# The query scratch as 16 long rows, and an exp that puts its scores back in order

## The chip, the cores and the metric

The kernel runs on one core of one Trainium2 chip. The metric is the device time of one execution in microseconds (us); lower is better. A core has five engines with queues of their own: PE (matmuls; its weight loads are shown as PEld), DVE (vector), ACT (activation functions), POOL (general purpose, and the issuer of DMAs that cast) and SP (here it only issues DMAs). Sixteen DMA engines serve all queues. The working memory SBUF and the matmuls' output memory PSUM both have 128 partitions.

## The reference, cut to what matters

Two steps follow one another. The first is an attention with pooled keys: `kv` is averaged over 4x4 squares, giving 768 rows per batch, and multiplied by `w_sr`; the result serves as keys and as values.

```python
kv_pool = kv.reshape(B, H // r, r, W // r, r, C).mean(axis=(2, 4))     # r = 4
k = v = kv_pool.reshape(B, -1, C) @ w_sr
s = q @ k.transpose(0, 2, 1) / sqrt(C)                                 # softmax over 768 keys
x = softmax(s) @ v
```

Here B = 4, C = 128, and q has 12,288 tokens per batch. The second step is a mixture of adapters on the 49,152 rows of x: a gate of 8 columns picks two experts per row with softmax weights, and each picked expert adds `w * (x @ A[e]) @ B[e]`, of rank 16.

## The kernel before

The 49,152 tokens are cut into 96 chunks of 512 (`k`), and four chunks make a group of 2048 tokens (`g`, 24 of them). Token p*16+j of a group (p from 0 to 127, j from 0 to 15) belongs to output partition p; chunk m of the group holds j = 4m to 4m+3. So every chunk is four blocks (`s`) of 128 tokens, and a store writes 2 KB in a row per partition.

For the scores PE needs q transposed: channels on the partitions, tokens along the row. Groups 0 and 1 are transposed by PE itself (`turn_q`). For groups 2 to 23, `cast_q(g)` (L78, its DMA on L80) has POOL issue a DMA that reads 1 MB of q in fp32 and writes it as bf16 into a scratch `qbf` in HBM, and `load_qT(g)` (L83, its DMA on L90) has SP issue a transposing DMA from the scratch into the tile `qT`; the last four groups go into a spare tile named `qTs`. Before the change the scratch is an image of q, [2048 tokens, 128], read as 128 rows of 2048 elements; the transpose leaves column j*128+p of `qT` for token p*16+j.

Per chunk there are three units (`scores(k, r)`, L286): two matmuls of 512 columns into one of two PSUM tiles `sg`, then one exp on ACT (L294) of 1024 elements per partition into `em` in fp16. `em[k]` has six blocks of keys (j) by 512 tokens. `attend(k, s)` (L296) then loads 128 tokens of `em` as weights, six times, and multiplies by the values `vx` into the single PSUM tile `acc`. DVE divides by the sum (`normalize`, L315 and L320, giving `xn`). DVE's MAX8 (`top`, L340) finds the two best experts, POOL works out the gates (`route`, L352 to L358; `gates`, L365 to L368, with a tanh on ACT and the tile `gw` as result), PE projects down (`h_ps`), DVE multiplies by the gates (`gate`, L420, giving `hg`), PE projects up (`d_ps`), DVE adds (`finish`, L433) and SP stores (L434). Between these, x and hg are transposed, by PE (`tt_ps`, copied to `tts` by DVE on L389) or, from chunk 68 on, by transposing DMAs on a tile `turn` (L407).

All engines keep the order in which the program is written. It is written in slots, one per chunk: an opening listed step by step in a string, then a loop from slot 8. `begin(k)` (L468) starts a slot: it calls `load_qT` where the table `loads` says so (slot 4g-6 for groups 4 to 17), `cast_q` where `casts` says so, and the loads of the next batch's `kv`. From slot 13 on a slot k computes the three score units of chunk k and attends chunk k-1. The casts and transposes of groups 2 and 3 belong to the opening's step `late` (`cast_first`, L449): POOL waits for an earlier load, casts both, and SP transposes both. In the opening, chunk 8, the first of group 2, is first used by the step `sc 8 0`, which follows `down 1` and precedes `at 4 2`.

All matmuls are recorded under one line, L69, that of the helper `mm`.

Of the kernel before, what the change touches and what calls it, by code (L numbers as in the profile page):

```python
# [11 lines left out]
BF16 = mybir.dt.bfloat16  # L12
U16 = mybir.dt.uint16
FP16 = mybir.dt.float16
AF = mybir.ActivationFunctionType
# [5 lines left out]
def kernel(  # L21
# [10 lines left out]
    nc = tc.nc  # L32
    P = 128
    B, N, C = q.tensor.shape
# [3 lines left out]
    J = NKV // P  # L38
    T = 512
    S = T // P  # L40
    GC = 4
    GT = GC * T
    VC = C + E - 1
    VE = VC + 1
    VP = 2 * C
    NB = N // T
    NCHUNK = B * NB
    scale = 1.0 / float(np.sqrt(C))
# [6 lines left out]
    ppool = ctx.enter_context(tc.tile_pool(name="ppool", bufs=8))  # L55
# [5 lines left out]
    qdram = ctx.enter_context(tc.tile_pool(name="qdram", bufs=1, space=bass.MemoryType.DRAM))  # L61
# [4 lines left out]
    keep = tc.keep_in_program_order  # L66

    def mm(*a, **k):
        return keep(nc.tensor.matmul(*a, **k))  # L69
# [5 lines left out]
    NG = N // GT  # L75
    q_bf, qT, kvr, spare = {}, {}, {}, {}

    def cast_q(g):  # L78
        t = qdram.tile([GT, C], BF16, tag=f"q{g}", name=f"qbf{g}")
        keep(nc.gpsimd.dma_start(t, q[g // NG, (g % NG) * GT:(g % NG + 1) * GT]))  # L80
        q_bf[g] = t

    def load_qT(g):  # L83
        if g < B * NG - GC:
            t = qpool.tile([P, GT], BF16, tag="qT", name="qT")
        else:
            if "q" not in spare:
                spare["q"] = kvpool.tile([P, 4, 2, 4 * C], FP32, tag="kvr", name="qTs")
            t = spare["q"][:, g % GC].rearrange("p x c -> p (x c)").bitcast(BF16)
        keep(nc.sync.dma_start(t.rearrange("c (j p) -> c j p", p=P),  # L90
                               q_bf[g].rearrange("(p j) c -> p (j c)", p=P), transpose=True))
        qT[g] = t


# [113 lines left out]
    kfT, vx = {}, {}  # L208
# [73 lines left out]
    em, acc, xn, xg, srt, gw = {}, {}, {}, {}, {}, {}  # L282
# [3 lines left out]
    def scores(k, r):  # L286
        b = k // NB
        if k not in em:
            em[k] = ppool.tile([P, J, T], FP16, tag="em", name="em")
        rhs = qT[k // GC][:, (k % GC) * T:(k % GC + 1) * T]  # L290
        ps = ps_s.tile([P, 2, T], FP32, tag="sg", name="sg")
        for i in range(2):
            mm(ps[:, i], kfT[b][:, 2 * r + i], rhs, start=True, stop=True)
        keep(nc.scalar.activation(em[k][:, 2 * r:2 * r + 2], ps, AF.Exp, bias=0.0, scale=scale))  # L294

    def attend(k, s):  # L296
        b = k // NB
        if s == 0:
            acc[k] = ps_a.tile([P, S, 256], FP32, tag="acc", name="acc")
        o = acc[k][:, s, 0:VE]  # L300
        for j in range(J):
            mm(o, em[k][:, j, s * P:(s + 1) * P], vx[b][:, j, 0:VE], start=(j == 0),
               stop=(j == J - 1))

    def attend_part(k, r):
        if r == 0:
            acc[k] = ps_a.tile([P, S, 256], FP32, tag="acc", name="acc")
        for s in range(S):
            for j in (2 * r, 2 * r + 1):
                mm(acc[k][:, s, 0:VE], em[k][:, j, s * P:(s + 1) * P], vx[k // NB][:, j, 0:VE],  # L310
                   start=(j == 0 and s % 2 == 0), stop=(j == J - 1 and s % 2 == 1))

    def normalize(k):
# [135 lines left out]
    def cast_first():  # L449
        keep(nc.gpsimd.tensor_copy(late, q_f[1, 2][:, 0, 0:1]))  # L450
        for g in (2, 3):
            cast_q(g)
        for g in (2, 3):
            load_qT(g)
# [3 lines left out]
    def unit(k=None, r=None):  # L458
        k, r = units.pop(0 if k is None else units.index((k, r)))
        scores(k, r)  # L460
# [7 lines left out]
    def begin(k):  # L468
        nonlocal sums, rest
        b, i = divmod(k, NB)  # L470
        g = k // GC
        if k in loads:
            load_qT(loads[k])
        if k in casts:
            cast_q(4 + casts.index(k))
        if b + 1 < B:
            lo = 3 if b == 0 else 0
            if i == lo:
                sums, rest = prepare(b + 1, nc.gpsimd)
                sums = sum(sums, [])  # L480
            if lo <= i < 12 + lo:
                load_kv(b + 1, (i - lo) // 4, (i - lo) % 4, None)
        if k == 7:
            for _ in range(2):
                sums.pop(0)()
# [11 lines left out]
    enter, t, left = {}, 1, list(range(NCHUNK - 3))  # L497
# [10 lines left out]
    def step(op, *w):  # L508
        v = [int(x) if x.isdigit() else engines.get(x, pools.get(x)) for x in w]
        if op == "T":  # L510
            turn_rows(v[0], 2 * (v[2] // 2) if w[1] == "s" else v[2],
                      v[2] % 2 if w[1] == "s" else v[3])
        elif op == "turn":
            turn_q(v[0] // GC, v[0] % GC, *v[1:])
        elif op in ("keys", "keys2", "values"):
            first_rest[v[0]][("keys", "keys2", "values").index(op)]()
        elif op == "gates":
            later.pop(0)()
        else:
            {"spin": spin, "proj1": project, "proj2": project2, "sum": add_rows, "sc": unit,  # L520
             "late": cast_first, "cast": cast_weights, "slot": begin, "at": attend, "atp": attend_part,
             "norm": normalize, "top": top, "route": route, "tr": transposes, "down": down,
             "gate": gate, "up": up, "fin": finish}[op](*v)
# [23 lines left out]
    for k in range(k1, NCHUNK):  # L547
        b, i = divmod(k, NB)
# [11 lines left out]
        if kx and not kd and all(x_ in by_dma for x_ in kx):  # L560
# [16 lines left out]
            for u_ in ku:  # L577
                up(u_)
                finish(u_)
            attend(ka[0], 0)  # L580
            attend(ka[0], 1)
            unit()
            for n in kn:
# [92 lines left out]
    def part(k, o, js):  # L676
        for s in range(S):
            for j in js:
                mm(o[:, s, 0:VE], em[k][:, j, s * P:(s + 1) * P], vx[k // NB][:, j, 0:VE],
                   start=(j == 0 and s % 2 == 0), stop=(j == J - 1 and s % 2 == 1))  # L680

    def wide(o):
# [40 lines left out]
    up_into(K - 4, bank(ps_m))  # L723
    o95 = bank(ps_s).rearrange("p a (b c) -> p (a b) c", c=256)
    part(K, o95, range(4))
    fetch(xT, K - 2)
    tanhs()
    down_into(K - 2, ps_m)
    carry(K - 4)
    normalize(K - 1)  # L730
    turn_x(K - 1, ps_m)
    part(K, o95, range(4, J))
    turn_h(K - 3, ps_a)
    fetch(xT, K - 1)
# [96 lines left out]
```

## Time and profile before

| what | value |
|---|---|
| median of 3 runs | 380.49 us (380.42 to 380.88) |
| profiled execution, span from first to last instruction | 379.1 us |
| PE busy | 368.8 us, 97% |
| DVE busy | 307.6 us, 81% |
| ACT busy | 293.3 us, 77% |
| POOL busy | 217.8 us, 57% |
| DMA moved | 82.22 MB in 93,863 packets |
| mean granted PE clock | 0.995 |

The profiled execution's own time is the span; the median of the runs is 1.4 us more, which lies around the span. A row of a group reads: line, engine, operation, out<-in with shapes, count, then busy time, mean time of one in ns, and idle time of the engine just before. A row of the timeline reads: start in us, length in us, engine, line, operation, count of merged instructions, and in brackets the idle time before it and what ended it. A row of the waits reads: who waited for whom, us in total, times, longest.

### The profile page before, as it was taken

Reading aid. Unit: us, or ns where it says so; the run is one execution under the profiler, and the core shown is the slowest. Engines: PE = TensorE matmul, PEld = TensorE weight load, DVE = VectorE, ACT = ScalarE, POOL = GpSimd, SP = SyncE. Lnnn points to the kernel's source line nnn. Section 1 sums busy time; section 2 is a strip of 40 time slices with the busy share of each in tenths; the row PEclk is TensorE's granted clock in tenths of the full one; section 3 lists DMA queues with packets and bytes.
Section 4 is the critical chain, followed back from the end, with each engine's and each line's share of the span. In section 5 each row is a group of like instructions: output and inputs, shape, how many; then the busy total and the mean of one; then the engine's idle time right before and its main releaser. Section 6 shows DMA issues by size and latency. Waiting matters only on the chain.

```text
span 379.1 us, 11473 instructions
## 1 busy us (share of the span) xinstructions
PE 368.8 (97%) x4448; PEld 292.5 (77%) x4448; DVE 307.6 (81%) x925; ACT 293.3 (77%) x368; POOL 217.8 (57%) x493
## 2 busy tenths in 40 slices
PE   8899999999999999999999999999999999999993
PEld 5577788788788887878788887878787777777782
DVE  1447799998989889898989888898988777777785
ACT  1448986776878788787878787777778999999873
POOL 0120468878732387777833267777675666666442
PEclk9999999999999999999999999999999999999998
DMA  7988979999999998997898998989955867777623
GB/s 247 388 291 151 279 184 266 340 224 241 152 213 228 299 278 268 255 235 165 171 201 226 288 239 245 306 233 198 217 137 140 169 163 153 150 205 168 141 86 140
DMA packets 93863, 82.22 MB, mean 217 GB/s; under 512 B 73104, under 2 KB 73872, under 8 KB 93456
## 3 DMA queue, kind: packets, MB, share of 16 engines
q1 hardware_dynamic: 92672, 69.75, 69.8%
q0 software_dynamic: 704, 11.54, 17.0%
q8 instruction: 35, 0.57, 0.6%
q10 hardware_dynamic: 432, 0.20, 0.2%
q14 instruction: 20, 0.16, 0.2%
HBM read 50.53 MB, written 36.70 MB: 230 GB/s over the span
## 4 chain that ended last, share of the span: by engine, by line
PE 91%; DMA 4%; DVE 2%; issue 1%; ACT 1%; SPq 0%; POOL 0%; ACTq 0%; DVEq 0%; POOLq 0%
PE acc L69 35%; PE sg L69 32%; PE tt_ps L69 8%; PE d_ps L69 5%; PE h_ps L69 5%; DMA kvr<-in_kv_dram 4%; PE kpT_ps L69 2%; PE v_ps L69 1%; DVE kvr L135 1%; DVE xn L320 1%; PE kfT_ps L69 1%; DMA out_dram<-osb 1%; PE qT_ps L69 0%; SPq L102 0%; PE tail_ps L69 0%
## 5 line engine op out<-in xcount | busy, mean ns | idle before, releaser
L294 ACT ACTIVATE em<-sg 128x1024 f16<-128x1024 f32 x288 | 282.4, 1022 | 66.8 <-PE sg L69 64.1
L69 PE MATMUL acc<-vx,em 128*128 128x136 f16 x2280 | 166.5, 223 | 0.0
L69 PEld LDWEIGHTS <-em 128*128 128x128 f16 x2304 | 145.2, 98 | 7.7 <-DVE xn L320 0.4
L69 PE MATMUL sg<-qT,kfT 128*128 128x512 bf16 x480 | 142.1, 379 | 0.8 <-ACT em L294 0.7
L320 DVE TENSOR_TENSOR xn<-acc,rinv 128x540 f32<-128x540 f32 x95 | 68.4, 720 | 3.3
L69 PEld LDWEIGHTS <-tts 128*128 128x128 bf16 x564 | 43.0, 98 | 31.6 <-issue 0.4
L223 POOL TENSOR_TENSOR kvr<-kvr 128x512 f32<-128x512 f32 x54 | 67.3, 1270 | 0.1
L352 POOL TENSOR_TENSOR over<-xn,srt 128x64 f32<-128x64 f32 (+1 forms) x120 | 30.9, 278 | 55.4 <-DVE srt L340 55.3
L433 DVE TENSOR_TENSOR osb<-d_ps,xn 128x512 f32<-128x512 f32 x91 | 62.5, 688 | 0.0
L420 DVE TENSOR_TENSOR hg<-h_ps,gw 128x512 bf16<-128x512 f32 x71 | 49.0, 691 | 6.3 <-POOL gw L368 1.2
L389 DVE COPY tts<-tt_ps 128x1024 bf16<-128x1024 bf16 (+1 forms) x73 | 49.0, 672 | 0.0
L69 PEld LDWEIGHTS <-kfT 128*128 128x128 bf16 x576 | 45.3, 98 | 2.7 <-issue 1.0
L315 DVE RECIPROCAL rinv<-acc 128x4 f32<-128x4 f32 x95 | 17.3, 182 | 36.9 <-PE acc L69 35.9
L367 POOL TENSOR_TENSOR gw<-th,over 128x64 f32<-128x64 f32 (+1 forms) x60 | 17.3, 288 | 49.6 <-ACT th L365 47.4
L69 PEld LDWEIGHTS <-xn 128*128 128x128 bf16 x296 | 22.5, 98 | 16.7 <-DVE xn L320 0.4
L340 DVE MAX8 srt<-xn 128x8 f32<-128x8 f32 x380 | 34.4, 152 | 0.1
L69 PE MATMUL sg<-qTs,kfT 128*128 128x512 bf16 x96 | 28.6, 379 | 0.0
L69 PE MATMUL tt_ps<-id_bf,xn 128*128 128x128 bf16 x284 | 27.4, 219 | 0.0
L69 PE MATMUL h_ps<-a_bf,tts 128*128 128x128 bf16 x284 | 27.4, 219 | 0.0
L69 PE MATMUL tt_ps<-id_bf,hg 128*128 128x128 bf16 x280 | 27.1, 219 | 0.0
L69 PE MATMUL d_ps<-b_bf,tts 128*128 128x128 bf16 x276 | 26.7, 219 | 0.1
L358 POOL TENSOR_SCALAR over<-over 128x64 f32<-128x64 f32 (+1 forms) x60 | 19.8, 330 | 5.4
(93 smaller groups left out, 280.7 us busy)
## 6 DMA issues: line engine op xcount, KB each, us to landing
out_dram<-osb SPq DMA_DIRECT2D x94, 256.0 KB, 4.3
kvr<-in_kv_dram SPq DMA_DIRECT2D x45, 512.0 KB, 7.8
qbf<-in_q_dram POOLq DMA_DIRECT2D x22, 512.0 KB, 7.7
qf<-in_q_dram SPq DMA_DIRECT2D x8, 256.0 KB, 7.4
kvr<-in_kv_dram SPq DMA_DIRECT2D x6, 256.0 KB, 7.8
out_dram<-osb SPq DMA_DIRECT2D x3, 128.0 KB, 2.3
turn<-turn SPq DMA_TRANSPOSE x23, 3.1
qT<-qbf SPq DMA_TRANSPOSE x18, 7.4
```

What stands on the lines that cost most here:

```text
L69: return keep(nc.tensor.matmul(*a, **k))
L223: keep(adder.tensor_tensor(u[:, lo:hi], u[:, lo:hi], v[:, lo:hi], op=ALU.add))
L294: keep(nc.scalar.activation(em[k][:, 2 * r:2 * r + 2], ps, AF.Exp, bias=0.0, scale=scale))
L315: keep(nc.vector.reciprocal(ri, acc[k][:, :, VC]))
L320: keep(nc.vector.tensor_tensor(x[:, :, 0:VC], acc[k][:, :, 0:VC], ri.unsqueeze(2).broadcast_to([P, S, VC]), op=ALU.mult))
L340: keep(nc.vector.max(srt[k0][:, m, s], xn[k][:, s, C:C + E]))
L352: keep(eng.tensor_tensor(d, lg, so[:, :, i].unsqueeze(2).broadcast_to([P, n, 8]), op=ALU.subtract))
L358: keep(eng.tensor_scalar(mask, mask, 0.0, None, op0=ALU.is_ge))
L367: keep(eng.tensor_tensor(w[:, 0:n], th, mask, op=ALU.mult))
L389: keep(nc.vector.tensor_copy(sb[:, lo:hi], ps[:, lo:hi]))
L420: keep(nc.vector.tensor_tensor(hg[k].rearrange("p s (e r) -> p (s e) r", e=E), hp[k].rearrange("p s (e r) -> p (s e) r", e=E), gw[k0][:, m ...
L433: keep(nc.vector.tensor_tensor(osb, dp[k], xn[k][:, :, 0:C], op=ALU.add))
```

## The change

The scratch is written in another order. It is a tile of 16 rows by 16,384 elements: row r holds the tokens whose p is r modulo 16, ordered by chunk m, then by p div 16 (`u`, 8 values), then by block s. The cast therefore writes pieces of 4 tokens, 512 elements. The transposing DMA reads these 16 rows in one instruction, and column (m, u, s, r) of `qT` holds the token. Within a chunk the 128 tokens of one block s no longer lie side by side, but in 8 runs of 16. The matmuls of the scores take the 512 columns as they come; the exp reads its PSUM tile in the order s, then key block and u, then r, and writes `em`, which now has the layout [s, key block, 128 tokens]. So `attend` loads the same 128 tokens as before, from another place in `em`. For groups 0 and 1, still transposed by PE, the exp reads whole blocks of 128 in the order s, key block.

```diff
     def cast_q(g):
-        t = qdram.tile([GT, C], BF16, tag=f"q{g}", name=f"qbf{g}")
-        keep(nc.gpsimd.dma_start(t, q[g // NG, (g % NG) * GT:(g % NG + 1) * GT]))
+        t = qdram.tile([16, GT // 16 * C], BF16, tag=f"q{g}", name=f"qbf{g}")
+        src = q[g // NG, (g % NG) * GT:(g % NG + 1) * GT].rearrange(
+            "(u r m s) c -> r m u (s c)", r=16, m=GC, s=S)
+        keep(nc.gpsimd.dma_start(t.rearrange("r (m u x) -> r m u x", m=GC, x=S * C), src))
         q_bf[g] = t
...
-        keep(nc.sync.dma_start(t.rearrange("c (j p) -> c j p", p=P),
-                               q_bf[g].rearrange("(p j) c -> p (j c)", p=P), transpose=True))
+        keep(nc.sync.dma_start(t.rearrange("c (m r) -> c m r", r=16), q_bf[g], transpose=True))
         qT[g] = t
...
     def scores(k, r):
         b = k // NB
         if k not in em:
-            em[k] = ppool.tile([P, J, T], FP16, tag="em", name="em")
+            em[k] = ppool.tile([P, S, J, P], FP16, tag="em", name="em")
...
-        keep(nc.scalar.activation(em[k][:, 2 * r:2 * r + 2], ps, AF.Exp, bias=0.0, scale=scale))
+        o = em[k][:, :, 2 * r:2 * r + 2]
+        if k // GC > 1:
+            o = o.rearrange("p s i (u r) -> p s (i u) r", r=16)
+            i_ = ps.rearrange("p i (u s r) -> p s (i u) r", s=S, r=16)
+        else:
+            i_ = ps.rearrange("p i (s t) -> p s i t", s=S)
+        keep(nc.scalar.activation(o, i_, AF.Exp, bias=0.0, scale=scale))
...
-            mm(o, em[k][:, j, s * P:(s + 1) * P], vx[b][:, j, 0:VE], start=(j == 0),
+            mm(o, em[k][:, s, j], vx[b][:, j, 0:VE], start=(j == 0),
                stop=(j == J - 1))
```

The two other places that load `em`, `attend_part` and `part`, change in the same way.

More of the change, by code (lines that the diff above doesn't have):

```diff
@@ L309, in attend_part @@
             for j in (2 * r, 2 * r + 1):
-                mm(acc[k][:, s, 0:VE], em[k][:, j, s * P:(s + 1) * P], vx[k // NB][:, j, 0:VE],
+                mm(acc[k][:, s, 0:VE], em[k][:, s, j], vx[k // NB][:, j, 0:VE],
                    start=(j == 0 and s % 2 == 0), stop=(j == J - 1 and s % 2 == 1))
@@ L678, in part @@
             for j in js:
-                mm(o[:, s, 0:VE], em[k][:, j, s * P:(s + 1) * P], vx[k // NB][:, j, 0:VE],
+                mm(o[:, s, 0:VE], em[k][:, s, j], vx[k // NB][:, j, 0:VE],
                    start=(j == 0 and s % 2 == 0), stop=(j == J - 1 and s % 2 == 1))
```

## The prediction

> **What bounds the kernel now.** I read the page's head first, then the busy time by stretch, then the waits, and last the timeline at the places that the change touches.
>
> ```profile
> span 379.1 us, 11473 instructions
> PE 368.8 (97%) x4448; PEld 292.5 (77%) x4448; DVE 307.6 (81%) x925; ACT 293.3 (77%) x368; POOL 217.8 (57%) x493
> DMA  7988979999999998997898998989955867777623
> ```
> ```profile
> core 0: us, PE busy (x) PEld busy (x) DVE busy (x) ACT busy (x) POOL busy (x), PEclk, DMA share, GB/s
> 27.00:60.00 33.00, 32.94 (x393) 26.23 (x392) 26.02 (x91) 28.36 (x35) 13.41 (x27) 1.00 0.83 217
> 60.00:284.00 224.00, 224.00 (x2836) 181.46 (x2834) 200.43 (x581) 173.95 (x209) 145.38 (x271) 1.00 0.99 233
> 284.00:356.00 72.00, 71.92 (x869) 55.80 (x867) 55.01 (x183) 67.28 (x89) 46.05 (x155) 1.00 0.72 162
> ```
> ```profile
> ACT em L294 <- PE sg L69: 52.4, 64, 1.3
> POOL gw L367 <- ACT th L365: 38.7, 32, 2.0
> DVE rinv L315 <- PE acc L69: 30.8, 70, 0.9
> ```
>
> From 27 to 356 us PE is busy in 328.86 of 329 us, at the full granted clock; the other engines wait for it (the last fence is the waits of 60 to 356 us; among them none is PE's own). The DMA engines are nearly as full (0.99 from 60 to 284 us), but nothing on PE waits for them there. The change takes no instruction from PE: the scores' matmuls read 512 neighbouring columns of qT as before, and the attend loads 128 neighbouring fp16 of em as before. So inside those 329 us nothing can be gained; the change can only be hidden or cost. The idle PE time lies ahead of 27 us, where only chunks turned by PE run, and behind 356 us, when all scratch has been read.
>
> **The exp.** It reads 1024 scores per partition in runs of 16 instead of in a row, and writes runs of 256.
>
> ```profile
> L294 ACT ACTIVATE em<-sg 128x1024 f16<-128x1024 f32 x288 | 282.4, 1022 | 66.8 <-PE sg L69 64.1
> L433 DVE TENSOR_TENSOR osb<-d_ps,xn 128x512 f32<-128x512 f32 x91 | 62.5, 688 | 0.0
> L420 DVE TENSOR_TENSOR hg<-h_ps,gw 128x512 bf16<-128x512 f32 x71 | 49.0, 691 | 6.3 <-POOL gw L368 1.2 <-PE kfT_ps L69 0.5
> ```
>
> No ACT instruction here reads in a permuted order. The nearest rows are DVE's: the gate multiply L420 walks its operands in runs of 16, one of them a repeated gw, and takes 691 ns for 512 elements; the plain add L433 takes 688. By that pair 3 ns per 512, so 6 ns per exp. The bounds: -0.02 us (an even walk over the two banks could save a little, nothing suggests more) to +0.25 us, if a run of 16 cost a quarter more; I take +0.01, the end that a measured pair supports. What a dearer exp costs is read where ACT is fullest.
>
> ```profile
> 202.85 2.85 ACT L294 ACTIVATE em<-sg 128x1024 f16<-128x1024 f32 x3 [0.61 <-PE sg L69]
> 204.04 0.59 PE L69 MATMUL sg<-qT,kfT 128*128 128x512 bf16 x2
> 305.87 3.15 ACT L294 ACTIVATE em<-sg 128x1024 f16<-128x1024 f32 x3
> 308.91 0.22 ACT L365 ACTIVATE th<-over 128x32 f32<-128x32 f32 x1
> 309.03 1.02 ACT L294 ACTIVATE em<-sg 128x1024 f16<-128x1024 f32 x1
> ```
>
> Three exps back to back take 2.85, so one starts (2.85-1.02)/2 = 0.915 us after the other. From 284 to 356 us a slot is 309.03-305.87 = 3.16 us and holds three exps and a tanh, 3x0.915+0.12 = 2.87 us: 0.29 us are free, 0.10 per exp. In the slots before, the first exp of a triple ends at 202.85+1.02 = 203.87, and the matmul that wants its PSUM buffer (there are two) starts at 204.04: 0.17 us free. So +0.01 us is hidden, and the price starts at about +0.10. Cost: 0.
>
> **The casts.** The 22 casts (L80) move the same bytes, but write 512 pieces of 1 KB, each from 2 KB of q.
>
> ```profile
> q1 hardware_dynamic: 92672, 69.75, 69.8%
> q0 software_dynamic: 704, 11.54, 17.0%
> ```
> ```profile
> L80 POOL DMA_DIRECT2D qbf<-in_q_dram x22: 504/577/755, 27.0 to 242.4; - x22
> ```
>
> The 704 packets of q0 are 32 per cast, two for each of 16 engines; I read them as one of data and one that ends it, so data goes from 16 pieces to 512. On the DMA engines a cast now holds 0.17x379.1/22 = 2.9 us of all sixteen. An engine gets 32 pieces for one; an average hardware packet, bytes included, is 0.698x16x379.1/92672 = 46 ns, so at most 1.5 us per cast, at least 0 (below it, if short pieces let other queues in sooner). Since that packet's bytes are already in the 2.9, I take a third, 0.5 us: 11 us in all, 3% of the span, on engines that PE does not wait for.
>
> On POOL the issue takes 577 ns, and what is queued behind it are the gates' steps, on which DVE's gate multiply waits.
>
> ```profile
> 95.06 0.36 POOL L358 TENSOR_SCALAR over<-over 128x64 f32<-128x64 f32 x1
> 95.38 0.57 POOL L80 DMA_DIRECT2D qbf<-in_q_dram  x1
> 95.97 0.33 POOL L367 TENSOR_TENSOR gw<-th,over 128x64 f32<-128x64 f32 x1
> 96.74 0.69 DVE L420 TENSOR_TENSOR hg<-h_ps,gw 128x512 bf16<-128x512 f32 x1 [0.27 <-POOL gw L368]
> ```
> ```profile
> 124.29 0.58 POOL L80 DMA_DIRECT2D qbf<-in_q_dram  x1
> 125.77 0.31 POOL L367 TENSOR_TENSOR gw<-th,over 128x64 f32<-128x64 f32 x1 [0.90 <-ACT th L365]
> ```
>
> At 124 us there are 0.90 us of cover, since gw waits for the tanh anyway; at 95 us there are none, and a longer issue goes straight to hg. DVE then has its own waits as cover: 30.8/70 = 0.44 us each. The price of 512 pieces is in no row. Ends: 0 (the 577 ns are a fixed cost) and 32x0.577 = 18.5 us (all of it per piece); I take +0.3 us, near the low end, because the time is the same within 504 to 755 ns for a megabyte read, which looks like a fixed cost. 0.3 is under the cover nearly everywhere: 0.
>
> A rule speaks against this. The Trainium skill, page "SBUF — State Buffer", section "Who interferes with whom", says that DVE in a two-port mode shuts GpSimd out for the whole instruction, and descriptor writing with it. With 32 times the pieces a cast would meet such an instruction more often. The trace shows no such stall so far: the longest of 22 issues is 755 ns with DVE busy for 200.43 of 224 us. By the rule, each cast that meets one DVE copy of 0.67 us takes 0.577+0.67 = 1.25 us, just inside the 1.3 us at which the rival on POOL's issue below begins at most casts, so the sum would stay 380.5; two copies would pass it.
>
> ```profile
> L389 DVE COPY tts<-tt_ps 128x1024 bf16<-128x1024 bf16 (+1 forms) x73 | 49.0, 672 | 0.0
> ```
>
> **The transposes.** The same 512 KB leave HBM through one instruction of 16 rows instead of 128.
>
> ```profile
> L90 SPq DMA_TRANSPOSE qT<-qbf x18: 2396/4782/6242, 33.2 to 268.1; - x18
> DMA to landing us min/median/max: 5.0/7.4/10.9
> ```
> ```profile
> L407 SPq DMA_TRANSPOSE turn<-turn x23: 1196/1239/2144, 283.5 to 355.6; - x23
> ```
>
> The least hold of SP is twice that of the half as large transposes of `turn` (2396 to 1196 ns), which have 128 rows of half the length: time goes by bytes here. With bytes unchanged I take the landing as unchanged, 7.4 us; bounds 5.0 (the fastest now) and 15 (twice the median). Behind it on SP wait stores and kv loads, none of which PE waits for. Is a later landing hidden? load_qT(g) is called six slots ahead of the first scores of its chunk 4g, 6x3.61 = 21.7 us (a slot is half of 207.38-200.16, two tanhs of even slots).
>
> ```profile
> 200.16 0.25 ACT L365 ACTIVATE th<-over 128x64 f32<-128x64 f32 x1
> 207.38 0.25 ACT L365 ACTIVATE th<-over 128x64 f32<-128x64 f32 x1
> ```
>
> Against a longest landing of 10.9 that leaves 10.8 us. Only group 2 is tight:
>
> ```profile
> 26.96 1.25 POOL L80 DMA_DIRECT2D qbf<-in_q_dram  x2
> 33.21 5.93 SPq L90 DMA_TRANSPOSE qT<-qbf  x2
> 42.23 0.39 PE L69 MATMUL h_ps<-a_bf,tts 128*128 128x128 bf16 x4
> 42.46 0.59 PE L69 MATMUL sg<-qT,kfT 128*128 128x512 bf16 x2
> ```
> ```profile
> qT<-qbf SPq DMA_TRANSPOSE x1, 6.3
> ```
>
> Issued at 33.21, its transpose lands 6.3 us later at 39.5; `sc 8 0`, the scores behind `down 1`, starts at 42.46. 3.0 us are free, against 0.3 us more on POOL (0.6 with the second cast's) and 0.5 on the engines. Hidden.
>
> **Sum.** 0 (exp) + 0 (casts) + 0 (transposes) on a span of 379.1 us. The median of the runs is 380.49, 1.4 us over the profiled span, which I take as what lies around it: 380.5 us. A difference under 0.2%, 0.76 us, is about what a measurement of this kernel can tell from none.
>
> **Rivals.**
>
> *The exp becomes dear* (chance 0.14; slower). It decides from +0.10 us per exp. At +0.15 the 22 slots from 284 to 356 us grow by 0.45-0.29 = 0.16 each: +3.5, 384.0. At +0.25 it is 22x0.46 = 10, and some 55 slots of 3.61 us lose 0.25-0.17 = 0.08 each, 4 more: 395. For it: no ACT row with such a walk exists. Against: the DVE pair.
>
> *POOL's issue grows* (0.12; slower). It decides from about 0.44 us at casts like that at 95 us, from 0.90+0.44 = 1.3 us elsewhere. At 2.5 us an issue, +1.9, twenty casts cost 0.6 each: 12, 392. For: 32 times the pieces. Against: the even 577 ns.
>
> *The first group comes late* (0.10; slower). It decides from 3.0 us, cast and transpose together, and is paid once: at +5 us, 382.5. For: both steps change and lie in series. Against: PE's next groups have three times that room.
>
> *The DMA engines become the bound* (0.06; slower). At twice the landing time the transposes alone need far more of engines that are at 0.99; with, say, a tenth of the 224 us overrun, 22, PE would wait at each group: 400. Against: bytes and rows' sums are the same.
>
> *Faster* (0.04). Only the 27 us of opening could give, through earlier kv loads: at most 1 us, 379.5. The 16-row form may well shorten SP's hold, but that is no time of PE.
>
> A transposed scratch that saves nothing on the DMA engines either (the change not doing what it is built for) gives the forecast too; it needs no case of its own.
>
> **How the numbers follow.** No change, as forecast, 0.54, within 379.8 to 381.2. Slower than 0.2%: 0.14+0.12+0.10+0.06 = 0.42. Faster: 0.04. For 8 in 10 the range takes in the forecast (0.54), the late group (0.10), and the lower halves of the exp's and POOL's cases (0.07 and 0.06) and half of the faster one: 379.8 to 389.
>
> **What would show it.** Right: exp at 1022 ns within 20; PE busy over 328 of the 329 us from 27 to 356; 22 casts on POOL under 1 us; landing of qT under 10.9 us. Wrong: "PE sg <- ACT em" or "PE sg <- DMA qT" among the waits, or gaps in PE's row after 60 us; the mean of L294 over 1.12 us names the exp, a POOL issue over 1.3 us the casts, a DMA share over 1 with a landing over 15 us the engines.

## The result, and the profile after

| what | before | after |
|---|---|---|
| median, same chip and hour | 380.69 us (14 of 18 runs) | 381.49 us (18 runs, 380.62 to 381.85) |
| ratio after/before, 95% interval | | 1.002 (1.0013 to 1.0027) |
| profiled execution, its time and its span | 380.88 and 379.1 us | 381.20 and 379.4 us |

Medians and ratios here and below leave out executions in a slower state of the chip (4 of 18 before), and the traces of e1 and e9 below, taken in that state, are read only ahead of the place where they fall behind.

The changed kernel is slower by 0.2%, some 0.8 us: just what a measurement of this kernel can tell from nothing. The forecast of 380.5 us was 1 us too low, and 0.2 us of that is the kernel before, which stood at 380.69 in that hour; the range held. The two profiled spans differ by only 0.3 us, because the execution of the changed kernel happened to begin its first exp 0.4 us earlier. First the page of the changed kernel: its head, its two large queues, the exp's group and two rows of the DMA issues.

```profile
span 379.4 us, 11473 instructions
PE 368.5 (97%) x4448; PEld 292.2 (77%) x4448; DVE 307.7 (81%) x925; ACT 293.5 (77%) x368; POOL 221.3 (58%) x493
...
DMA packets 60071, 82.22 MB, mean 217 GB/s; under 512 B 28048, under 2 KB 40080, under 8 KB 59664
...
q1 hardware_dynamic: 47968, 69.75, 62.9%
q0 software_dynamic: 11616, 11.54, 21.4%
...
L301 ACT ACTIVATE em<-sg 128x1024 f16<-128x1024 f32 x288 | 282.6, 1022 | 67.1 <-PE sg L69 64.4
...
qbf<-in_q_dram POOLq DMA_DIRECT2D x22, 512.0 KB, 9.2
...
qT<-qbf SPq DMA_TRANSPOSE x18, 6.4
```

The exp is L301 now and takes 1022 ns, as it did. The transposes' queue q1 went from 92,672 packets to 47,968 and from 69.8% to 62.9% of the engines' time: 0.069 x 379 = 26 us less. The casts' queue q0 went the other way, from 704 packets to 11,616 and from 17.0% to 21.4%, 17 us more. Its 11,616 packets are 528 per cast, 512 of data and 16 that end it, as the prediction had read them. The next two fences are the changed kernel's casts (tile `qbf`) and transposes (tile `qT`), which answer to L80 and L90.

```profile
L82 POOL DMA_DIRECT2D qbf<-in_q_dram x22: 692/698/866, 26.9 to 242.6; - x22
```
```profile
L92 SPq DMA_TRANSPOSE qT<-qbf x18: 1831/4304/6955, 34.5 to 265.5; - x18
...
DMA to landing us min/median/max: 4.3/6.4/11.6
```

A cast costs POOL 698 ns instead of 577. Then PE's row by stretch, in the prediction's columns, and those of the changed kernel's waits from 27 to 366 us in which PE waits for something that it did not wait for before.

```profile
27.00:60.00 33.00, 32.64 (x390) 25.70 (x389) 25.98 (x91) 28.22 (x35) 13.87 (x27) 1.00 0.84 212
60.00:284.00 224.00, 223.81 (x2832) 181.21 (x2830) 200.12 (x580) 173.88 (x209) 147.97 (x270) 1.00 0.95 233
284.00:356.00 72.00, 71.92 (x872) 55.95 (x870) 55.05 (x183) 67.19 (x90) 46.47 (x156) 1.00 0.70 162
```
```profile
PEld qT_ps L69 <- ACT qT L127: 0.8, 1, 0.8
...
PEld kpT_ps L69 <- POOL kvr L222: 0.4, 1, 0.4
PE qT_ps L69 <- ACT qT L127: 0.3, 1, 0.3
...
PE kpT_ps L69 <- POOL kvr L222: 0.2, 1, 0.2
```

PE's busy time in those 329 us fell from 328.86 to 328.37, and it fell in two places, each a single wait. Both stand in code that the diff does not touch. The starts of the 288 exps show that there is no third place in these two traces: set against the kernel before, the changed kernel's exps start 0.01 to 0.02 us later from the 14th to the 66th, and 0.25 to 0.27 us later from the 67th to the last.

**Place 1, at 30 us.** PE transposes group 1's four chunks itself (`qT_ps`). Here are the timelines around the first three, with ACT's copy of the second and, before, DVE's copy of the first; before first, then after.

```profile
28.62 0.60 PE L69 MATMUL qT_ps<-id_f,qf 128*128 128x128 f32 x4
...
29.26 0.69 DVE L128 CAST qT<-qT_ps 128x512 bf16<-128x512 f32 x1 [0.66 <-PE qT_ps L69]
...
29.49 0.60 PE L69 MATMUL qT_ps<-id_f,qf 128*128 128x128 f32 x4
...
30.65 0.59 ACT L126 CAST qT<-qT_ps 128x512 bf16<-128x512 f32 x1
...
30.83 0.60 PE L69 MATMUL qT_ps<-id_f,qf 128*128 128x128 f32 x4
```
```profile
28.12 0.60 PE L69 MATMUL qT_ps<-id_f,qf 128*128 128x128 f32 x4
...
28.99 0.60 PE L69 MATMUL qT_ps<-id_f,qf 128*128 128x128 f32 x4
...
30.14 0.59 ACT L127 CAST qT<-qT_ps 128x512 bf16<-128x512 f32 x1
...
30.79 0.65 PE L69 MATMUL qT_ps<-id_f,qf 128*128 128x128 f32 x4 [0.30 <-ACT qT L127]
```

Before, the third chunk's transposes begin at 30.83 while ACT still copies the second out (30.65 to 31.24). After, they wait for that copy's end (30.14 + 0.59 = 30.73) and begin at 30.79: 1.80 us behind the second instead of 1.34. The pool `ps_m` has two PSUM banks, and the kernel asks only for one of them (`mtile`); which it gets is settled when the program is built. In the built program before, the pool's 27th tile, this one, has the bank that DVE had emptied by 29.26 + 0.69 = 29.95; in the changed one it has the bank that ACT is emptying. All of PE's instructions and their order are the same in both.

**Place 2, at 100 us.** POOL's timeline between the cast of slot 20 and the last sums of pooled keys for batch 1, and PE's row that uses them (`kpT_ps`); before, then after.

```profile
95.97 0.33 POOL L367 TENSOR_TENSOR gw<-th,over 128x64 f32<-128x64 f32 x1
96.39 0.32 POOL L368 TENSOR_TENSOR gw<-gw,over 128x64 f32<-128x64 f32 x1
96.66 1.27 POOL L223 TENSOR_TENSOR kvr<-kvr 128x512 f32<-128x512 f32 x1
98.01 2.07 POOL L221 TENSOR_TENSOR kvr<-kvr 128x512 f32<-128x512 f32 x2
...
100.14 0.44 PE L69 MATMUL kpT_ps<-id_f,kvr 128*128 128x128 f32 x2
```
```profile
95.51 0.69 POOL L82 DMA_DIRECT2D qbf<-in_q_dram  x1
96.22 0.33 POOL L374 TENSOR_TENSOR gw<-th,over 128x64 f32<-128x64 f32 x1
96.63 0.32 POOL L375 TENSOR_TENSOR gw<-gw,over 128x64 f32<-128x64 f32 x1
96.91 1.27 POOL L224 TENSOR_TENSOR kvr<-kvr 128x512 f32<-128x512 f32 x1
98.26 2.08 POOL L222 TENSOR_TENSOR kvr<-kvr 128x512 f32<-128x512 f32 x2
...
100.39 0.44 PE L69 MATMUL kpT_ps<-id_f,kvr 128*128 128x128 f32 x2 [0.18 <-POOL kvr L222]
```

The casts of slots 19 and 20 both stand on POOL ahead of these sums. Each is 0.12 us longer, the sums end 0.25 us later, and PE's `kpT_ps` begins 0.25 us later. The sums end at 98.01 + 2.07 = 100.08 before, and PE begins at 100.14: there was no slack to begin with.

### The profile page after: what moved, and what is told of

The parts are those of the page before. It is cut to its first block, busy times and chain, and to the rows that moved or that the text cites. A ratio compares the mean times of both kernels' runs of the same rounds, so it can differ in the third digit from the quotient of the medians.

```text
span 379.4 us, 11473 instructions
## 1 busy us (share of the span) xinstructions
PE 368.5 (97%) x4448; PEld 292.2 (77%) x4448; DVE 307.7 (81%) x925; ACT 293.5 (77%) x368; POOL 221.3 (58%) x493
## 3 DMA queue, kind: packets, MB, share of 16 engines
q1 hardware_dynamic: 47968, 69.75, 62.9%
q0 software_dynamic: 11616, 11.54, 21.4%
## 4 chain that ended last, share of the span: by engine, by line
PE 86%; DMA 4%; POOL 3%; DVE 2%; issue 1%; ACT 1%; SPq 0%; ACTq 0%; POOLq 0%; DVEq 0%
PE acc L69 34%; PE sg L69 30%; PE tt_ps L69 8%; PE d_ps L69 5%; PE h_ps L69 5%; DMA kvr<-in_kv_dram 4%; PE kpT_ps L69 2%; POOL kvr L224 1%; PE v_ps L69 1%; DVE kvr L136 1%; DVE xn L327 1%; DMA out_dram<-osb 1%; PE kfT_ps L69 1%; POOL kvr L222 1%; ACT em L301 1%
## 5 line engine op out<-in xcount | busy, mean ns | idle before, releaser
L301 ACT ACTIVATE em<-sg 128x1024 f16<-128x1024 f32 x288 | 282.6, 1022 | 67.1 <-PE sg L69 64.4
```

The lines of the kernel that those rows point to most:

```text
L301: keep(nc.scalar.activation(o, i_, AF.Exp, bias=0.0, scale=scale))
```

## The experiments

Two distances in the traces tell the two places apart in every kernel. **A** is the time from the start of group 1's second `qT_ps` to that of its fourth (4.28 us before, 4.80 after; the third, which waits, lies between). **B** is the time from the start of the 65th exp to that of the 67th, between which the `kpT_ps` at 100 us lies (3.07 us before, 3.31 after). The differences, 0.52 and 0.24, make 0.76 us of the 0.8 measured.

| kernel | A | B | median us | ratio to before, 95% interval |
|---|---|---|---|---|
| before | 4.28 | 3.07 | 380.59 / 380.54 / 380.0 in the three sets | |
| after | 4.80 | 3.31 | 381.49 | 1.002 (1.0013 to 1.0027) |
| e1 exp only | 4.28 | 3.06 | 380.59 | 1.0003 (0.9990 to 1.0016) |
| e2 scratch only | 4.80 | 3.28 | 381.49 | 1.0024 (1.0013 to 1.0034) |
| e3 cast moved | 4.80 | 2.92 | 381.10 | 1.0012 (0.9999 to 1.0026) |
| e4 kv first | 4.80 | 3.28 | 381.43 | 1.0024 (1.0013 to 1.0035) |
| e5 banks | 4.28 | 3.33 | 380.78 | 1.0005 (0.9996 to 1.0015) |
| e6 banks, cast moved | 4.28 | 2.91 | 380.26 | 0.9990 (0.9981 to 0.9999) |
| e7 before, new banks | 4.80 | 3.07 | 381.41 | 1.0034 (1.0011 to 1.0058) |
| e8 before, cast moved | 4.28 | 2.92 | 380.47 | 0.9998 (0.9988 to 1.0007) |
| e9, e10 rows | 4.28 | 3.06, 2.92 | 399.08, 397.96 | 1.0490, 1.0492 |

e1 to e4 share one set of runs of the kernel before, e5 to e8 another, e9 and e10 a third; the row "after" goes by the set of the result, where the kernel before took 380.69.

**e1 and e2: which half.** e1 has the new layout of `em` and the permuted exp beside the old scratch; since the old `qT` isn't in runs of 16, its rows come out in another order. e2 has the new cast and transpose beside the old exp, so its rows are out of order too.

```diff
# e1, from the kernel after: cast_q and load_qT as before
...
-        src = q[...].rearrange("(u r m s) c -> r m u (s c)", r=16, m=GC, s=S)
+        keep(nc.gpsimd.dma_start(t, q[g // NG, (g % NG) * GT:(g % NG + 1) * GT]))
...
# e2, from the kernel before: cast_q and load_qT as after
-        keep(nc.gpsimd.dma_start(t, q[g // NG, (g % NG) * GT:(g % NG + 1) * GT]))
+        src = q[...].rearrange("(u r m s) c -> r m u (s c)", r=16, m=GC, s=S)
...
```

> Leaves out the new scratch: cast and transpose as before, new layout of em and the permuted exp (its pairs of tokens and scores are then not the reference's). POOL theory (each cast holds POOL 0.12 us longer, two casts ahead of the last key sums): no difference from before, within 0.1%, exp at 1022 ns, PE's gap ahead of kpT at 100 us as before (0.11 us over a plain matmul). Rival, the exp costs something that only other executions show: 0.1 to 0.2% slower.

> Leaves out the new exp: new cast and transpose, em and exp as before (tokens stay permuted). POOL and SP theories: the whole loss, 0.1 to 0.25% slower than before, casts at 0.70 us on POOL, last sums 0.25 us later or more, kpT at 100 us late by as much. Rival exp: no difference.

e1 took 380.59 us and e2 381.49, beside 380.59 of the kernel before: the whole loss is the scratch's, and no cost of the exp shows.

**e3 and e4: whose delay.** At this point I knew of place 2, not of place 1. e3 moves the cast of slot 19 to slot 21, behind the key sums. e4 puts the loads of `kv` ahead of the transpose and the cast in `begin`, since SP waits ahead of a transpose until the cast has landed (21.7 us in four waits in the changed kernel).

```diff
# e3
-    casts = sorted([k for k in range(8, 61, GC)] + [15, 19, 23, 39, 43, 47])
+    casts = sorted([k for k in range(8, 61, GC)] + [15, 21, 23, 39, 43, 47])
# e4: in begin(k) the block "if b + 1 < B: ... load_kv(...)" goes ahead of
#     "if k in loads: load_qT(...)" and "if k in casts: cast_q(...)"
```

> The changed kernel with the cast of slot 19 moved to slot 21, so that one cast and not two stands ahead of the last key sums on POOL. POOL theory: sums earlier by 0.7 us, the wait of kpT at 100 us gone, at least 0.25 us back, so equal to before within 0.05% or faster. Rival, late kv loads (SP waits for longer casts, the last kv load of batch 1 lands at 87.7 instead of 84.2 us, and in other executions later than the 88.5 us at which its sums begin): the same loss mostly stays where the landing is late by more than 0.7 us, but small delays are absorbed too.

> The changed kernel with each slot's kv load issued ahead of its transpose and cast instead of behind. Theory of late kv loads: kv of batch 1 lands 3 us earlier, the part of the loss that the profile does not show (0.4 us of the 0.76) comes back, 0.05 to 0.1% slower than before is left by POOL. POOL theory alone: no gain, 0.2% slower as in the changed kernel.

e4 changed nothing (381.43): late loads are not the cause. e3 came to 381.10, 0.39 us less than e2 in the same set, and B fell from the changed kernel's 3.31 to 2.92, by the same 0.39. This B is 0.15 below that of the kernel before. The expected return to the time before did not come. In e3 POOL's sums end at 97.59 + 2.08 = 99.67 and PE begins at 99.82; the rows are e3's timeline.

```profile
97.59 2.08 POOL L222 TENSOR_TENSOR kvr<-kvr 128x512 f32<-128x512 f32 x2
...
99.82 0.39 PE L69 MATMUL kpT_ps<-id_f,kvr 128*128 128x128 f32 x2
```

Now PE comes last there, with 0.15 us to spare. That left some 0.5 us open against the kernel before, and all four traces showed where: e2, e3 and e4, all three with the new scratch, have A at 4.80, and e1 has it at 4.28.

**e5 to e7: the bank.** e5 gives the changed kernel the bank order of the kernel before, e7 gives the kernel before that of the changed one, e6 is e5 with the cast of slot 19 moved as in e3.

```diff
# e5 and e6 (from after); e7 (from before) has [26, 260, 320]
-    ps_m = ctx.enter_context(tc.tile_pool(name="ps_m", bufs=2, space=bass.MemoryType.PSUM))
+    ps_m = ctx.enter_context(tc.tile_pool(name="ps_m", bufs=1, space=bass.MemoryType.PSUM))
...
-        return ps_m.tile(shape, dtype, tag="mb", name=name)
+        turns[0] += 1
+        n = turns[0] + sum(turns[0] > i for i in [260, 320])
+        return ps_m.tile(shape, dtype, tag=f"mb{n % 2}", name=name)
```

The list says after which tiles a bank is taken twice in a row; the program before does so after the 260th and 320th, the changed one after the 26th too.

> The changed kernel, with the two PSUM banks of the pool ps_m taken in the order in which the kernel before takes them (tile 27 of the pool, group 1's third transposed chunk, then waits for DVE's old cast and not for ACT's fresh one). Theory 'a bank': the 0.46 us that this transpose waits in the changed kernel (29.0 to 30.8 us where it was 29.5 to 30.8) is a loss of its own at the opening; the third qT_ps comes 1.34 us after the second instead of 1.80, the wait for ACT's qT goes, the time falls by 0.4 to 0.5 us to about 381.0. Rival 'the opening is hidden': the wait is swallowed by PE's later waits before 42 us; the time stays at 381.4 to 381.5. The late key sums at 100 us stay in both: +0.2 to 0.25.

> The same, and the cast of slot 19 moved to slot 21 as well. Theory 'two losses, a bank and the key sums': both come back, 381.49 - 0.46 - 0.39 = 380.6, the time of the kernel before (380.63) within 0.1, with no PE wait for POOL's kvr at 100 us and none for ACT's qT at 30 us. Rival 'there is a third loss, in the casts' greater use of the DMA engines': 380.9 or more.

> The kernel before (old scratch, old transposes, old exp), with the two banks of ps_m taken in the order of the changed kernel: tile 27 of the pool takes the bank that ACT has just read. Theory 'a bank': the wait of 0.46 us comes without any of the change, 380.63 + 0.4 to 0.5 = 381.05 to 381.1, and the third qT_ps begins 1.8 us after the second. Rival 'the opening is hidden': 380.6.

All three went the way of the bank theory, each by 0.2 to 0.4 us more than its figure (380.78 for 381.0, 380.26 for 380.6, 381.41 for 381.1). The fences are the PE timelines of e5 and e7 at group 1's second and third transposes.

```profile
29.10 0.60 PE L69 MATMUL qT_ps<-id_f,qf 128*128 128x128 f32 x4
...
30.45 0.60 PE L69 MATMUL qT_ps<-id_f,qf 128*128 128x128 f32 x4
```
```profile
29.32 0.60 PE L69 MATMUL qT_ps<-id_f,qf 128*128 128x128 f32 x4
...
31.12 0.66 PE L69 MATMUL qT_ps<-id_f,qf 128*128 128x128 f32 x4 [0.30 <-ACT qT L130]
```

With the old banks the changed kernel has no wait and takes 380.78 us; what is left to 380.54 is 0.24, as much as the key sums' 0.24, though the interval of this time alone holds 1. With the new banks the kernel before, otherwise untouched, has the wait and takes 381.41. That is 0.87 us more where A says 0.52; the interval, 0.4 to 2.2 us, holds 0.52, and what the rest is, if anything, the runs do not settle. e6 takes both losses away and comes to 380.26, so no third loss is left in the engines' greater use by the casts. In the profiled executions of e5 and e6 the exps fall back once more, by 0.45 and 0.31 us at 355 us, where PE or its weight load waits for a DMA on `turn`. By then the last cast is over 100 us old and no transpose of the scratch is left, and the kernel before and the changed kernel have no such wait; whether other executions of e5 and e6 have it is not known.

**e8: the kernel before, cast moved.**

```diff
# from the kernel before
-    casts = sorted([k for k in range(8, 61, GC)] + [15, 19, 23, 39, 43, 47])
+    casts = sorted([k for k in range(8, 61, GC)] + [15, 21, 23, 39, 43, 47])
```

> The kernel before with the cast of slot 19 moved to slot 21, past the last key sums. Theory 'the key sums have no slack, before either': PE passes 100 us 0.15 us earlier than in the kernel before, as in the changed kernel with the cast moved, and the time is 380.45 to 380.5. Rival 'the kernel before has cover there': 380.6, PE's steps at 100 us unchanged.

B is 2.92 and the median 380.47: the kernel before lost 0.15 us to the key sums already. 0.15 us is less than times can show here (the interval holds 1), and only the trace shows it. The fastest version is e6, 380.26, at a ratio of 0.9990 (0.9981 to 0.9999): 0.3 us, of which 0.15 is this cast's place; the rest lies within the interval.

**e9 and e10: 16 rows without the 512 pieces.** Scratch row r can also hold 128 tokens that follow one another. Then the cast is the old one, the transpose takes 16 rows, the exp reads in runs of 16 as in the kernel after, and the output store has to put the tokens right. e10 is e9 with the cast of slot 19 moved.

```diff
# from the kernel after, with the old cast_q
-        keep(nc.sync.dma_start(t.rearrange("c (m r) -> c m r", r=16), q_bf[g], transpose=True))
+        src = q_bf[g].rearrange("(r x) c -> r (x c)", r=16)
+        keep(nc.sync.dma_start(t.rearrange("c (x r) -> c x r", r=16), src, transpose=True))
...
+    def dest(k):
+        rows = out[k // GC * GT:(k // GC + 1) * GT]
+        if k // GC > 1:
+            return rows.rearrange("(r m u s) c -> m u r s c", r=16, m=GC, s=S)[k % GC]
...
```

> The 16-row transpose without the 512-piece cast: scratch row r holds the 128 consecutive queries r*128 and on (the old cast, 16 pieces), the transpose takes 16 rows, the exp reads in the permuted order, and the permutation that is then left (partition p = 16u + r is query 128r + 32m + 4u + s) is undone in the output stores, in pieces of 2 KB as before. Theory 'both losses come from the cast': the cast takes 577 ns on POOL as before, the banks of ps_m come out as in the kernel before, the third qT_ps begins 1.34 us after the second, PE makes no step at 100 us, and the time is that of the kernel before, 380.6 within 0.2, with some 44,000 packets fewer on q1. Rival 'the 16-row transpose or the permuted exp has a price of its own': 380.9 or more.

> The same with the cast of slot 19 moved to slot 21. Theory 'the key sums bound PE at 100 us in every version': PE passes 100 us 0.15 us earlier than in the kernel before, the time is 380.45 or a little less, as of the kernel before with that cast moved (380.47). Rival 'fewer packets in the queue help as well': 380.2, as of the changed kernel with its banks in the old order and the cast moved (380.26).

On the time both theories were wrong, by 18 to 19 us (e10's profiled execution took 395.15 us). On the two places the first was right: A is 4.28, B 3.06 and 2.92, and the 201st exp starts within 0.5 us of the kernel before's place. So the bank's swap and the long issue both come with the 512-piece cast, and neither the 16-row transpose nor the permuted exp has a price on PE's path up to there. What can have cost the time is the one other part that I had changed, the stores, though no run has them alone. Here are the rows of the tile `out_dram` of e10, and its PE waits from 267 to 366 us, where PE did not wait for `turn` in the kernel before.

```profile
L446 SPq DMA_DIRECT2D out_dram<-osb x91: 337/607/2082, 48.2 to 375.6; - x91
L708 SPq DMA_DIRECT2D out_dram<-osb x4: 603/790/1960, 384.5 to 388.1; - x4
L717 SPq DMA_DIRECT2D out_dram<-osb x2: 603/604/604, 381.0 to 383.8; - x2
```
```profile
PE h_ps L69 <- DMA turn<-turn: 8.2, 3, 7.1
```

The last rows are bare issues: 603 ns for a store whose partitions go to 8 x 16 places. The row of the kernel before that answers to the last of them is:

```profile
L711 SPq DMA_DIRECT2D out_dram<-osb x2: 332/332/333, 370.5 to 373.4; - x2
```

From chunk 68 on PE needs transposes by DMA (`turn`), issued by SP between those stores, and from 267 us on it waits for them. SP issues the first of them at 290.14 us in e10 and at 283.51 in the kernel before, although POOL has its input ready at 283.0 us in e10. These 6.6 us are nearly all of the longest wait, 7.1 us. From 255 us on SP has no pause in e10, and each transpose of the scratch holds it for 4.3 to 4.8 us, where it took 2.1 to 4.1 before. So this wait is SP's time; why those transposes hold SP longer beside these stores was not tried.

## Why the prediction was right or wrong

- **The bound, and "can only be hidden or cost": right.** The criterion "PE busy over 328 of the 329 us" was met, by 328.37, and was too coarse: the half microsecond that it let pass is most of the loss. Another sign that the prediction named did appear: a gap in PE's row after 60 us, the 0.18 us at 100 us.
- **The exp at 0: right.** 1022 ns forecast within 20, 1022 measured; e1 shows no cost in the time (1.0003, 0.9990 to 1.0016).
- **The casts on POOL at 0: the failed step.** The size was overstated, +0.3 us taken, +0.12 measured (577 to 698 ns). The cover was misread. At 95 us I followed the issue to `gw` and from there to DVE's gate multiply, granted DVE 0.44 us, and stopped. The next two rows of the same timeline are the key sums, whose reader is PE itself, 0.06 us behind. So POOL's rival decides from 0 there, not from 0.44: its mechanism happened, at 0.24 us and not at 12.
- **What the working did not have at all: the bank.** It listed instructions, waits and queues of the changed code. The larger loss, 0.52 us, comes from a tile that the diff does not name and that was placed on another bank when the program was built. The program swaps the bank when it is built with the new cast alone; e9, with the 16-row transpose and the old cast, keeps the old order. By which rule it is chosen was not looked into.
- **The casts on the engines: right in sign, mis-sized.** 0.5 us per cast taken, (0.214 - 0.170) x 379 / 22 = 0.76 measured, inside the bound of 1.5; the landing went from 7.7 to 9.2. It costs nothing, as forecast: e6 has it and is not slower than the kernel before.
- **The transposes "unchanged": wrong, without effect.** "Time goes by bytes" failed: with the same bytes SP's least hold fell from 2396 to 1831 ns, q1 lost 26 us of engine time and 44,704 packets, and the landing of `qT` fell from 7.4 to 6.4. A longest landing of 11.6 us overstepped the 10.9 named as the mark of "right"; the cover of 21.7 us held.
- **Group 2: right.** Its transpose, issued at 34.45, landed at 39.86, and its first use came at 42.47.
- **The rule of the Trainium skill** ("SBUF — State Buffer", "Who interferes with whom"): with 32 times the pieces the longest issue grew from 755 to 866 ns, so no cast had a whole DVE copy of 0.67 us on top. That is no test of the rule: by the same section a copy enters a two-port mode only when its operands meet certain conditions, and the copy that I took for one, `tts` from `tt_ps`, reads PSUM. In which mode it runs, no run here shows. I also set an issue's length, 1.25 us, against a lengthening, 1.3 us; the term was +0.67.
- **The time around the span.** I set the median of the runs, 380.49, against the span of another run. The profiled run took 380.88 itself, so 1.8 us lie around the span; after it is 381.20 - 379.4, 1.8 too.
- **The chances.** 0.54 for "same" and 0.42 for "slower" were set by four large prices, none of which came at its size. What came were two small ones at the edge between the two, for which there was no case: 381.49 lies just above the 381.2 up to which "no change" went. That the range held is owed to its width, 8 us upward for prices that stayed away, and not to a right account of the casts and the banks.

## What to carry to other kernels

Where one engine has no gaps, follow every lengthened instruction down its queue until a reader on that engine is met, or until a wait longer than the lengthening; the first reader is not the only one. After any edit, compare which buffer each tile got and what each instruction waits for, also in code that was not edited: a swapped bank costs like an added instruction, and can be put back. A loss under 0.3% is found by the distance between two landmarks close together on the bounding engine, which among kernels with the same place agreed to 0.05 us here, where the times of whole runs scatter by 1 us.

## What the runs showed of the hardware

- A transposing DMA that reads 16 rows of 32 KB moves in few, long packets: in the DMA records 352 packets of 32 KB, 16 per transpose, stand in place of 45,056 of 256 B, 2048 per transpose from 128 rows of 4 KB. They hold the engines for 54 us instead of 79 at the same bytes.
- A cast to 512 pieces costs POOL 0.12 us more than one to 16: 698 against 577 ns. By this pair the issue is nearly all fixed cost, 0.24 ns a piece.
- The exp reads PSUM in runs of 16 and writes in runs of 256 at the speed of a plain one, 1022 ns for 1024 elements per partition.
- The issue of a 256 KB store on SP takes 603 ns with its partitions in two dimensions of HBM (8 x 16) and 332 with them in one.
